# Local attention of layer B: second scores in full PSUM banks, and P times V on 64-key row halves into two banks

## The chip, the cores and the metric

One core of one Trainium2 chip runs the whole program in one launch. The metric is device time in microseconds (us); the median of three runs is given, and one further execution was profiled.

## The reference

Two independent attention layers, each with S = 2048 positions, D = 1024, 32 heads of 32 columns, fp32. Layer A attends to 8 positions at a distance of 2. Layer B is a sliding block:

```
q, k, v = split(x @ wqkv)                        # 32 heads of 32
scores = einsum("bhqd,bhkd->bhqk", q, k) * 32 ** -0.5
mask = (q_idx - k_idx >= 0) & (q_idx - k_idx < 256)
p = softmax(where(mask, scores, -1e9))
o = einsum("bhqk,bhkd->bhqd", p, v)
return o @ wo
```

Both results are concatenated. A query of layer B sees itself and the 255 keys before it.

## The kernel before

The work is cut into eight units of 512 positions: units 0 to 3 are layer B ("dense" in the code), units 4 to 7 layer A. All units but the first of layer B have a halo: the last 256 keys of the unit before. A unit has eight head groups of four heads. Projections (queries and keys L576, values L641, output L702) are accumulations of 24 matmuls in the split of fp32 into a high and a low fp32r part (three products for each of 8 slices); their PSUM banks come from the ring `g`.

For a head group of layer B the scores are computed twice. The first scores (L923, queries on the PSUM partitions) give the maximum and the sum of each row: VectorE masks and takes the maximum (L928), ScalarE exponentiates and sums (L933). Maximum and logarithm of the sum go as an additional row into the stacked queries (L962, L968), so that the second scores (`second`, L1005, keys on the PSUM partitions) come out of exp as finished probabilities. A key block `kb` of 128 keys (-2 to 3, where -2 and -1 are the halo) meets 128, 256 or 384 queries. One bank holds one head's 384 columns, or two heads' 256 or 128; exp (`expo`, L1012) takes a bank to `pbuf` in SBUF, and `keep` zeroes the parts outside the window, on GpSimd (L991) or VectorE (L994), whichever the plan finds earlier. The six key blocks are dealt in two lots, because `pbuf` holds one lot.

P times V (`values`, L1052) follows each lot: plain fp32 matmuls with 128 keys as rows and 32 columns of V, four heads side by side on four column tiles of 32 columns, all accumulating in one bank `o`. After the second lot `finish` splits `o` into a high part (ScalarE, L888) and a low part (VectorE, L892) in the tile `ot`, which the output projection reads one unit later. Layer A's scores and P times V (L772, L838) are computed in a similar way on small tiles.

PSUM has eight banks: `g` 3, scores `s` 4 (`NS`), `o` 1.

The order on every engine is written by a planner inside the kernel. `Clock` keeps the planned end of each engine; four sequences (`gemm`, `ones` for first scores, `twos` for second scores and P times V, `aux`) wait side by side, and the main loop always emits the item whose planned readiness is earliest. Tables steer it: `PACE` (one row for each unit: delays and biases), `V_AT` and `O_AT` (at which head group value parts and output projections of the unit before are placed), `EDGE_AT` with `EDGES_V` (where weights and inputs of the next unit are split at a unit's edge). Weights stream through `raw` buffers by transfers that GpSimd issues (L166), and ScalarE and VectorE split them (L216, L219, L222).

Of the kernel before, what the change touches and what calls it, by code (L numbers as in the profile page):

```python
# [31 lines left out]
PACE = ((0.1, 1.2, 0.1, 0.0, 0.0, -99, 2), (0.2, 1.2, 0.0, 0.0, 0.2, -99, 1), (0.2, 1.2, 0.0, 0.0, 0.0, -99, 2), (0.2, 0.6, 0.0, 0.0, 0.2, -99, 2), (4.0, 7.0, 0.5, 0.0, 1, 2), (4.0, 7.0, 1.5, 0.5, 1, 1), (4.0, 7.0, 0.5, 0.2, 1, 3), (4.0, 7.0, 0.5, 0.0, 1, 2))  # L32
V_AT = ({1: 0, 3: 1, 7: 2}, {0: 0, 5: 1, 7: 2}, {0: 0, 5: 1, 7: 2}, {0: 0, 5: 1, 7: 2}, {0: 0, 5: 1, 7: 2}, {0: 0, 6: 1, 7: 2}, {0: 0, 5: 1, 7: 2}, {0: 0, 5: 1, 7: 2})
O_AT = ({2: (0, 1), 3: (2, 3), 4: (4, 5), 5: (6, 7)}, {2: (0, 1), 3: (2, 3), 4: (4, 5), 5: (6, 7)}, {2: (0, 1), 3: (2, 3), 4: (4, 5), 5: (6, 7)}, {2: (0, 1), 3: (2, 3), 4: (4, 5), 5: (6, 7)}, {2: (0, 1), 3: (2, 3), 4: (4, 5), 5: (6, 7)}, {2: (0, 1), 3: (2, 3), 4: (4, 5), 5: (6, 7)}, {1: (0, 1), 2: (2, 3), 3: (4, 5), 4: (6, 7)}, {2: (0, 1), 3: (2, 3), 4: (4, 5), 6: (6, 7)})
EDGE_AT = (0, 3, 0, 1, 0, 0, 2, 0)
EDGES_V = (
# [207 lines left out]
def kernel(ctx, tc, xs, wqk, wv, wo, outs, units):  # L244
# [175 lines left out]
    class Ring:  # L420
        def __init__(self, pool, n, tag):
            self.pool, self.n, self.tag = pool, n, tag
            self.free = [0.0] * n
            self.i = 0

        def when(self, late=0.0):
            t = self.free[self.i % self.n]
            return t and t + late

        def take(self):  # L430
            i = self.i % self.n
            self.i += 1
            self.free[i] = None
            return self.pool.tile([P, 512], F32, tag=self.tag, name=self.tag), i
# [4 lines left out]
        def empty(self):  # L439
            return None if None in self.free else max(self.free)  # L440

    rg, rs, ro = Ring(psg, 7 - NS, "g"), Ring(pss, NS, "s"), Ring(pso, 1, "o")
# [159 lines left out]
    def v_items(u, part):  # L602
# [64 lines left out]

        for r in range(len(rounds)):
            for n in range(len(rounds[r])):
                for k in range(kw):  # L670
                    for b in range(2):
                        at = (r, n, k, b)
                        out.append((lambda at=at: ready(*at), lambda at=at: run(*at), 3 * (CG if wide else CV),
                                    lambda at=at: after(*at)))
# [223 lines left out]


    def attention(u, s):  # L900
# [80 lines left out]
        kbs = [(-2, 0, 128, 2), (-1, 0, 256, 2)] if has_halo else []  # L981
        kbs += [(0, 0, 384, 1), (1, 128, 384, 1), (2, 256, 256, 2), (3, 384, 128, 2)]
        nk = len(kbs)
        lots = [(0, 1, 2), (3, 4, 5)] if has_halo else [(0, 1), (2, 3)]
        lot = {k: i for i, ks in enumerate(lots) for k in ks}
        at = {k: sum(kbs[i][2] for i in ks if i < k) for ks in lots for k in ks}
# [10 lines left out]
        def second(ki, hp):  # L997
            kb, q0, n, pack = kbs[ki]
            heads = list(range(hp * pack, hp * pack + pack))
            pr = heads[0] // 2  # L1000
            if heads[0] % 2 == 0:
                h["left", ki, pr] = 2 // pack
            ps, bank = rs.take()
            for i, j in enumerate(heads):
                nc.tensor.matmul(ps[:, i * n:(i + 1) * n], kk[:, j, 256 + kb * P:256 + (kb + 1) * P],  # L1005
                                 q[:, j, q0:q0 + n], start=True, stop=True)
            w = pbuf[:, heads[0]:heads[0] + pack, at[ki]:at[ki] + n]
            if ki == nk - 1 and hp == 4 // pack - 1:
                free_keys(hg)

            def expo():
                nc.scalar.activation(w, ps[:, :pack * n].rearrange("p (j n) -> p j n", j=pack),  # L1012
                                     AF.Exp)
                e = ck.use("act", pack * n / 1200 + 0.055, ck.now, pfree[0])
                rs.give(bank, e)

                def masks():
                    r = e
                    if kb >= 0:
                        r = max(r, keep(w[:, :, 0:P], cst["keep_d"], P, pack, 1, 0, -1, e))  # L1020
                    if kb < 2:
                        r = max(r, keep(w[:, :, n - P:n], cst["keep_f"], P, pack, -1, -1, 1, e))
                    h["left", ki, pr] -= 1
# [186 lines left out]
```

## Time and profile before

| | us |
|---|---|
| median of three runs | 1806.58 (1804.88 to 1807.36) |
| span of the profiled execution | 1803.3 |
| TensorE busy in it | 1788.7 |
| VectorE, ScalarE, GpSimd busy | 1229.5, 1036.7, 386.9 |

No separate time of the profiled execution is listed beside its span; the median lies 3.3 us above the span. The profile has rows by source line, engine and operation with their count, busy time and the mean of one; "PE" is TensorE's matmul, "PEld" its weight loads, DVE VectorE, ACT ScalarE, POOL GpSimd. A timeline merges neighbours of one line: start, length, count. An answer by windows counts the instructions that touch a stretch of time.

### The profile page before, as it was taken

To read this page: it belongs to the slowest core of one execution; us is meant where nothing else is said; L and a number is where in the kernel's file an instruction comes from. 1 tells how busy PE (TensorE), PEld (TensorE's weight loads), DVE (VectorE), ACT (ScalarE), POOL (GpSimd) and SP (SyncE) were. 2 spreads that over 40 slices of the span, in tenths; PEclk is the share of its full clock that TensorE was granted. 3 is DMA by queue.
4 is the path that set the end of the run, shared out by engine and by line. 5 is a ranking of instruction groups with operands and counts; after the bars stand their busy time and mean duration, and the time that the engine had idled before them with its cause. 6 is when DMAs were issued, how large, how long until landed. Compare 5 with 4: busy or idle time off the path is not lost.

```text
span 1803.3 us, 34584 instructions
## 1 busy us (share of the span) xinstructions
PE 1788.7 (99%) x12778; PEld 1462.7 (81%) x12778; DVE 1229.5 (68%) x2631; ACT 1036.7 (57%) x2643; POOL 386.9 (21%) x905
## 2 busy tenths in 40 slices
PE   8999999999999999999999999999999999999999
PEld 6787877888787788787888788878888888888887
DVE  6677875657766668666676486686677566866673
ACT  5667667665766665766677364453445344634452
POOL 3222223232232223323233300110001100100000
PEclk9999999999999999999999999999999999999999
DMA  8355665545546455554544433433334443533332
GB/s 243 115 151 136 184 167 148 170 130 172 160 135 177 139 152 176 139 155 134 153 137 138 128 125 125 140 126 135 128 112 151 142 135 113 159 129 135 126 105 82
DMA packets 109129, 257.20 MB, mean 143 GB/s; under 512 B 14496, under 2 KB 29856, under 8 KB 108960
## 3 DMA queue, kind: packets, MB, share of 16 engines
q0 software_dynamic: 41760, 152.06, 26.6%
q1 hardware_dynamic: 56832, 83.00, 17.3%
q10 hardware_dynamic: 10368, 19.93, 3.0%
q8 instruction: 101, 1.65, 0.4%
q14 instruction: 68, 0.56, 0.1%
HBM read 164.63 MB, written 23.07 MB: 104 GB/s over the span
## 4 chain that ended last, share of the span: by engine, by line
PE 94%; DMA 2%; ACT 2%; DVE 2%; issue 0%; POOL 0%; ACTq 0%; SPq 0%; DVEq 0%
PE g L576 38%; PE g L702 19%; PE g L641 18%; PE s L1005 6%; PE s L923 5%; PE o L1052 5%; PE o L838 2%; PE s L772 1%; DMA kst<-nat 1%; DMA halo<-nat 1%; ACT qst L968 1%; DVE s L928 0%; DVE w L222 0%; DMA raw<-xs 0%; ACT kst L391 0%; DMA qst<-nat 0%
## 5 line engine op out<-in xcount | busy, mean ns | idle before, releaser
L576 PE MATMUL g<-x,w 128*128 128x512 f32 x3072 | 763.7, 393 | 2.4 <-ACT x L216 1.3
L576 PEld LDWEIGHTS g<-x,w 128*128 128x128 f32 x3072 | 567.1, 188 | 111.5 <-issue 3.2
L641 PE MATMUL g<-w,x 128*128 128x256 f32 (+1 forms) x2304 | 390.0, 320 | 1.3 <-DVE w L222 1.2
L928 DVE CUSTOM_DVE_ANT_0 s<-s,mask_d 128x384 f32<-128x384 f32 (+2 forms) x512 | 263.2, 553 | 153.5 <-PE s L923 152.3
L222 DVE TENSOR_TENSOR w<-raw,w 128x512 fp32r<-128x512 f32 x516 | 336.6, 694 | 41.1 <-ACT w L216 34.6
L641 PEld LDWEIGHTS g<-w,x 128*128 128x128 f32 x2304 | 333.0, 190 | 30.6 <-DVE w L222 3.2
L702 PE MATMUL g<-ot,w 128*128 128x512 f32 x1416 | 344.0, 393 | 0.9 <-ACT ot L888 0.7
L933 ACT ACTIVATE s<-s,nm 128x384 f32<-128x384 f32 (+2 forms) x512 | 273.5, 535 | 75.0 <-DVE nm L928 72.7
L702 PEld LDWEIGHTS g<-ot,w 128*128 128x128 f32 x1416 | 261.8, 188 | 56.1 <-issue 1.8
L991 POOL TENSOR_SCALAR_AFFINE_SELECT pbuf<-pbuf 128x128 f32<-128x128 f32 (+1 forms) x574 | 205.9, 386 | 267.7 <-ACT pbuf L1012 263.7
L1012 ACT ACTIVATE pbuf<-s 128x384 f32<-128x384 f32 (+2 forms) x480 | 199.5, 506 | 54.7 <-PE s L1005 51.7
L219 DVE CAST w<-raw 128x1024 fp32r<-128x1024 f32 x189 | 130.8, 692 | 76.7 <-PE g L576 44.4
L166 POOL DMA_DIRECT2D raw<-wqk x126 | 68.7, 545 | 458.9 <-DVE w L222 315.8
L923 PE MATMUL s<-kst,qst 96*128 96x384 f32 (+2 forms) x512 | 144.5, 342 | 2.2 <-DMA kst<-nat 1.8
L1005 PEld LDWEIGHTS s<-qst,kst 128*128 128x128 f32 x704 | 108.9, 189 | 36.0 <-ACT s L933 13.2
L1005 PE MATMUL s<-qst,kst 128*128 128x256 f32 (+2 forms) x704 | 132.1, 303 | 1.4 <-ACT qst L968 1.0
L820 ACT COPY wide<-wide 32x256 f32<-32x256 f32 x256 | 103.4, 404 | 38.3 <-DVE wide L811 34.9
L923 PEld LDWEIGHTS s<-kst,qst 96*128 96x128 f32 x512 | 92.4, 188 | 27.2 <-issue 8.1
L166 POOL DMA_DIRECT2D raw<-wv x72 | 46.4, 644 | 279.7 <-DVE w L222 167.9
L933 ACT ACTIVATION_READ_ACCUMULATOR s<-s,nm 128x1 f32 x512 | 104.7, 205 | 0.2
L166 POOL DMA_DIRECT2D raw<-wo x64 | 36.1, 564 | 295.2 <-DVE w L222 158.2
L594 ACT COPY ost<-g 128x512 f32<-128x512 f32 x44 | 25.8, 586 | 120.2 <-PE g L702 120.2
(79 smaller groups left out, 1399.4 us busy)
## 6 DMA issues: line engine op xcount, KB each, us to landing
raw<-wqk POOLq DMA_DIRECT2D x126, 512.0 KB, 3.7
raw<-wv POOLq DMA_DIRECT2D x72, 512.0 KB, 4.2
raw<-wo POOLq DMA_DIRECT2D x64, 512.0 KB, 3.9
qst<-nat SPq DMA_DIRECT2D x96, 256.0 KB, 3.8
kst<-nat SPq DMA_DIRECT2D x96, 256.0 KB, 4.0
raw<-xs POOLq DMA_DIRECT2D x28, 512.0 KB, 4.5
outs<-ost ACTq DMA_DIRECT2D x56, 256.0 KB, 2.2
kst<-halo SPq DMA_DIRECT2D x72, 128.0 KB, 2.7
```

The costliest lines, as they stand in the source:

```text
L166: (self.nc.scalar if early else self.nc.gpsimd).dma_start(raw if len(ap.shape) == 2 else raw.rearrange("p (a b) -> p a b", a=2), ap)
L219: nc.vector.tensor_copy(t[:, 0, :], raw)
L222: nc.vector.tensor_tensor(t[:, 1, c:c + 512], raw[:, c:c + 512], t[:, 0, c:c + 512].bitcast(F32), op=ALU.subtract)
L576: nc.tensor.matmul(h["ps"], h["w"][:, a, k * P:(k + 1) * P], xt[u][k][:, b, :], start=(k == 0 and i == 0), stop=(k == NK - 1 and i == 2))
L641: nc.tensor.matmul(ps, xt[u][kw * g + k][:, a, p0:p0 + P], h["w"][g][:, c, k], start=(first and t == 0 and half == 0), stop=(last and t == 2),
L702: nc.tensor.matmul(h["ps"], w[:, a, c:c + P], ot[u, k][:, b, :], start=(k == 0 and i == 0), stop=(k == NK - 1 and i == 2))
L923: nc.tensor.matmul(ps[:, :n], q[0:96, j, b * P:(b + 1) * P], kk[0:96, j, c0:c1], start=True, stop=True)
L928: nc.vector.tensor_tensor_reduce(ps[:, :n], ps[:, :n], mask[:, cut:full], scale=-1.0, scalar=BIG, op0=ALU.add, op1=ALU.min, accum_out=nm)
L933: nc.scalar.activation(ps[:, :n], ps[:, :n], AF.Exp, bias=nm, scale=-1.0, accum_out=sm)
L991: nc.gpsimd.affine_select(w, w, pattern=[[0, m], [step, n]], compare_op=ALU.is_ge, fill=0.0, base=base, channel_multiplier=chan)
L1005: nc.tensor.matmul(ps[:, i * n:(i + 1) * n], kk[:, j, 256 + kb * P:256 + (kb + 1) * P], q[:, j, q0:q0 + n], start=True, stop=True)
L1012: nc.scalar.activation(w, ps[:, :pack * n].rearrange("p (j n) -> p j n", j=pack), AF.Exp)
```

## The change

`second` now fills whole banks: for a head, the 128 or 384 columns of two key blocks stand next to each other in one bank of 512 (blocks -2 and 0 in the first lot, 3 and 1 in the second), and the 256 columns of two heads share a bank (block 2 in the first lot, block -1 in the second). One exp covers a bank. Where two masked squares of 128 columns of one kind lie in the bank, one mask instruction covers both by a strided view. The number of matmuls and their columns stay.

`values` works on 64 keys at a time: the row half r (keys 0 to 63 or 64 to 127 of a block) uses rows 64r to 64r+63 of the array, covers only the 320 query columns that its keys can see (fewer at the edges), and accumulates in a bank of its own (`o` for r = 0, `x` for r = 1). A list alternates the halves so that both get the same number of columns; heads 0 and 1 go through the whole list first, then heads 2 and 3. `join` replaces `finish` in layer B: ScalarE copies `x` into `pbuf` (the columns of head 3), VectorE adds `o`, then ScalarE and VectorE split the sum as before. The last exp of the next group's first lot, which is head 3's, is planned behind that.

The ring `g` has two banks while layer B runs; at its end the bank of `x` joins it. The value projection lets its second bank lag by two steps in layer B (`SKEW`), so that the two banks finish at different times. The planner's cost of P times V follows the new columns. The tables have new entries: `PACE` in units 1 to 5 and 7, `V_AT` in unit 4, `O_AT` in units 4 and 6, `EDGE_AT` in units 1 to 4, two rows of `EDGES_V`; `LAG7` is used by no unit.

```diff
-LAG7, LAG0 = 1, 3
+LAG7, LAG0 = 0, 3
+SKEW = 2
...
-EDGE_AT = (0, 3, 0, 1, 0, 0, 2, 0)
+EDGE_AT = (0, 1, 2, 0, 1, 0, 2, 0)
...
-    psg = ctx.enter_context(tc.tile_pool(name="psg", bufs=7 - NS, space=PSUM))
+    psg = ctx.enter_context(tc.tile_pool(name="psg", bufs=2, space=PSUM))
+    psx = ctx.enter_context(tc.tile_pool(name="psx", bufs=1, space=PSUM))
...
+        skew = SKEW if units[u][2] else 0
         for r in range(len(rounds)):
+            steps = [(n, k) for n in range(len(rounds[r])) for k in range(kw)]
+            for i in range(len(steps) + skew):
+                for b in range(2):
+                    if 0 <= i - skew * b < len(steps):
+                        at = (r,) + steps[i - skew * b] + (b,)
...
+    def join(u, s, h):
...
+        both = pbuf[:, 3, :S]
+        nc.scalar.copy(both, h["o"][1])
...
+            nc.vector.tensor_tensor(both, h["o"][0], both, op=ALU.add)
...
+                nc.scalar.copy(o[:, 0, :], both)
...
+                    nc.vector.tensor_tensor(o[:, 1, :], both, o[:, 0, :].bitcast(F32), op=ALU.subtract)
...
-        lots = [(0, 1, 2), (3, 4, 5)] if has_halo else [(0, 1), (2, 3)]
+        lots = [[((0, 128, 384),), ((2, 512, 256),)], [((3, 0, 128), (1, 128, 384))]]
+        if has_halo:
+            lots = [[((-2, 0, 128), (0, 128, 384)), ((2, 512, 256),)], [((3, 0, 128), (1, 128, 384)), ((-1, 512, 256),)]]
+        lots = [[(segs, (j,)) for j in range(3) for segs in lot[:1]] +
+                [(segs, (j, j + 1)) for j in (0, 2) for segs in lot[1:]] +
+                [(segs, (3,)) for segs in lot[:1]] for lot in lots]
...
             for i, j in enumerate(heads):
+                for kb, c, w in segs:
+                    q0 = max(0, kb * P)
+                    x = i * n + c - c0
+                    nc.tensor.matmul(ps[:, x:x + w], kk[:, j, 256 + kb * P:256 + (kb + 1) * P], q[:, j, q0:q0 + w],
+                                     start=True, stop=True)
...
+                for r in range(2):
+                    a, b = max(0, kb * P + 64 * r if has_halo or kb else 0), min(S, kb * P + 64 * r + 320)
+                    p.append((b - a, r, kb, a, c + a - q0))
+            rows_of = [sorted(x for x in p if x[1] == r) for r in range(2)]
+            out, t = [], [0, 0]
+            while rows_of[0] or rows_of[1]:
+                r = 0 if rows_of[0] and (not rows_of[1] or t[0] <= t[1]) else 1
+                out.append(rows_of[r].pop())
+                t[r] += out[-1][0]
...
-                for j in range(4):
-                    nc.tensor.matmul(h["o"][32 * j:32 * j + 32, q0:q0 + n],
-                                     v[:, slot, vc + 32 * j:vc + 32 * j + 32], pbuf[:, j, at[ki]:at[ki] + n],
-                                     start=(ki == 0), stop=(ki == nk - 1), skip_group_check=True)
+            for j0 in (0, 2):
+                for n, r, kb, q0, c in pieces[li][0]:
+                    slot = (4 * u + kb) % 6
+                    part = slice(64 * r, 64 * r + 64)
+                    for j in (j0, j0 + 1):
+                        nc.tensor.matmul(h["o"][r][32 * j:32 * j + 32, q0:q0 + n],
+                                         v[part, slot, vc + 32 * j:vc + 32 * j + 32], pbuf[part, j, c:c + n],
+                                         start=(j, r) not in h["begun"], stop=True, skip_group_check=True)
```

More of the change, by code (lines that the diff above doesn't have):

```diff
@@ L995, in keep, with second @@
             return ck.use("dve", dur_d, r, port=True)
[L997 to L1002, printed above, removed]
+        def second(li, ci):
+            segs, heads = lots[li][ci]
+            m = len(heads)
+            c0, n = segs[0][1], sum(x[2] for x in segs)
             ps, bank = rs.take()
             for i, j in enumerate(heads):
[L1005 to L1008, printed above, removed]
+                for kb, c, w in segs:
[3 more added lines that the diff above has]
+                                     start=True, stop=True)
+            w = pbuf[:, heads[0]:heads[0] + m, c0:c0 + n]
+            if li == 1 and ci == len(lots[1]) - 1:
@@ new lines, in attention @@
+        for lot in lots:
+            p = []
+            for kb, c, w in [x for segs, heads in lot for x in segs if heads[0] == 0]:
+                q0 = max(0, kb * P)
+                for r in range(2):
[7 more added lines that the diff above has]
+                t[r] += out[-1][0]
+            pieces.append((out, max(t)))
```

127 lines of the change are left out of this document (70 added, 57 removed), and 4 rows, old and new, of the table EDGES_V.

## The prediction

> **What bounds the kernel now.** I read the page's busy times first, then busy time by stage, then the chain of waits.
>
> ```profile
> span 1803.3 us, 34584 instructions
> PE 1788.7 (99%) x12778; PEld 1462.7 (81%) x12778; DVE 1229.5 (68%) x2631; ACT 1036.7 (57%) x2643; POOL 386.9 (21%) x905
> PE 94%; DMA 2%; ACT 2%; DVE 2%; issue 0%; POOL 0%; ACTq 0%; SPq 0%; DVEq 0%
> ```
> ```profile
> core 0: us, PE busy (x), PEclk, DMA share, GB/s
> 0.00:45.00 45.00, 39.63 (x163) 1.00 0.81 242
> 45.00:1030.00 985.00, 980.09 (x6005) 1.00 0.52 149
> 1030.00:1803.00 773.00, 769.01 (x6613) 1.00 0.39 128
> ```
>
> TensorE is busy 99% of the span at the full granted clock (1.00), and 94% of the chain is its own work. Layer B ends about 1030 us. Between 45 and 1030 us TensorE idles 985.0 - 980.1 = 4.9 us, in layer A 4.0 us. No other engine is a bound on average. So the change must be costed as TensorE time that goes or comes, plus a few microseconds of waits. The span is 1803.3 us; the median of the runs is 1806.58, 3.3 us above it, and I add that 3.3 to every sum.
>
> **Part 1, P times V.** This is the only part that changes TensorE's work: the first scores, the second scores (same 704 matmuls, same columns), and the projections keep their matmuls.
>
> ```profile
> 63.66 1.50 PE L1052 MATMUL o<-pbuf,vbuf 128*32 128x384 f32 x16
> 70.40 0.86 PE L1052 MATMUL o<-pbuf,vbuf 128*32 128x256 f32 x16
> 406.32 1.50 PE L1052 MATMUL o<-pbuf,vbuf 128*32 128x384 f32 x24
> ```
>
> Each source matmul is two MATMULs (704 in the loop, 1408 in the trace), and four heads run side by side on four column tiles. In the first unit the burst at 63.66 us has 384+384 = 768 columns for each head, the one at 70.40 has 256+128 = 384. The slope is (1.50 - 0.86)/384 = 1.67 ns per column for four heads together. Each of the 48 lots in units with a halo (24 head groups, two lots) has 768 columns, as the third row; the 8 groups of the first unit have 768+384 = 1152.
>
> After the change a piece covers 64 keys and only the 320 columns that those keys can see. By the greedy list, each row half gets 640 columns a lot with a halo, and 576+448 = 1024 for a group without. If both row halves and all four heads run at once, a lot with a halo falls from 768 to 640 columns, 128 x 1.67 = 0.21 us, times 48 is 10.2 us; the first unit gains 128 x 1.67 x 8 = 1.7 us. That is the good end: -11.9 us.
>
> But the loop does heads 0 and 1 through the whole list before heads 2 and 3. If only the four tiles of one pair ran at a time, a lot would take 2 x 640 columns: +512 x 1.67 = 0.85 us, times 48 is 41.0, and the first unit (2048 - 1152) x 1.67 x 8 = 11.9: +52.9 us, the bad end. What decides is how far the array looks past matmuls that wait for their own tile. The nearest rows are those of the scores of layer A, 32 source matmuls on eight tiles (32 rows by 64 columns), in one burst, counted from its start:
>
> ```profile
> 1080.03:1080.13 0.10, 0.10 (x8) 0.10 (x11) 1.00 0.96 266
> 1080.03:1080.23 0.20, 0.20 (x18) 0.20 (x26) 1.00 1.15 297
> 1080.03:1080.33 0.30, 0.30 (x27) 0.30 (x33) 1.00 0.97 280
> 1080.03:1080.39 0.36, 0.36 (x33) 0.36 (x34) 1.00 1.00 302
> 1080.03:1080.48 0.45, 0.45 (x38) 0.45 (x41) 1.00 0.97 305
> 1080.03:1080.63 0.60, 0.60 (x52) 0.60 (x58) 1.00 0.91 304
> 1080.03:1080.98 0.95, 0.95 (x64) 0.80 (x64) 1.00 0.84 295
> ```
> ```profile
> L772 PE MATMUL s<-pbuf x2048: 221/221/272, 1034.4 to 1750.8; 32*64 32x72 f32 x187
> ```
>
> The first column in brackets is MATMULs begun, the second weight loads. Eight begin within 0.10 us, one on each tile: eight tiles in four row groups and two column groups do run together. 33 loads have begun by 0.30 us, and then only one more by 0.36: after 16 source matmuls (32 loads, 32 MATMULs) the stock in front of the array is used up and the rest is fed as earlier ones finish. Eight rounds of 72 columns need 8 x 72 x 0.83 = 0.48 us (0.83 is half the slope, for one of the two MATMULs); the burst took 0.95, and 0.73 without the last MATMUL's own 0.22. So what lies beyond the first 16 cost 0.25 us here.
>
> In a lot with a halo of the changed kernel, heads 0 and 1 make 12 source matmuls and heads 2 and 3 the next 12. The stock of 16 reaches the first four of the second pair, so all eight tiles start, but the list outruns it. I charge the same 0.25 us to each of the 48 lots: -0.21 + 0.25 = +0.04, +1.9 us in all. The first unit's lots have 16 source matmuls and are not charged: -1.7 us. Sum: **+0.2 us**, with -11.9 and +52.9 as ends. Entering and leaving the small tiles happens twice a group as before. The sum trusts that the 0.25 comes from the queue and not from the tile size.
>
> *A rule that speaks against the change.* Twice as many MATMULs must be fed. From 0.36 to 0.60 us the rows count 52 - 33 = 19 MATMULs, 12.6 ns each; 96 of them are 1.2 us, less than the 1.32 us of a lot in my sum, so by the rows feeding adds nothing. The Trainium skill, TensorE: Matmul & The Clock Gate, section Back-to-back issue gap, gives a floor of about 25 ns for each MATMUL however small; by it a lot of 96 would take 2.4 us and the kernel would end some 64 us later (an estimate from that page). This trace disagrees with the floor for tiles that run together.
>
> **Part 2, exp, masks and the join.**
>
> ```profile
> L1012 ACT ACTIVATE pbuf<-s 128x384 f32<-128x384 f32 x256 | 108.1, 508 | 33.5 <-PE s L1005 33.0
> L1012 ACT ACTIVATE pbuf<-s 128x512 f32<-128x512 f32 x112 | 63.2, 610 | 12.6 <-PE s L1005 10.6 <-POOL pbuf L991 1.3
> L1012 ACT ACTIVATE pbuf<-s 128x256 f32<-128x256 f32 x112 | 39.1, 396 | 8.6 <-PE s L1005 8.1 <-POOL pbuf L991 0.5
> L991 POOL TENSOR_SCALAR_AFFINE_SELECT pbuf<-pbuf 128x128 f32<-128x128 f32 x397 | 129.2, 354 | 125.0 <-ACT pbuf L1012 122.9 <-PE s L1005 0.8
> L991 POOL TENSOR_SCALAR_AFFINE_SELECT pbuf<-pbuf 128x256 f32<-128x256 f32 x177 | 77.8, 456 | 142.7 <-ACT pbuf L1012 140.8
> L888 ACT CAST ot<-o 128x512 fp32r<-128x512 f32 x64 | 37.5, 587 | 98.2 <-PE o L1052 56.1 <-PE o L838 41.6
> L892 DVE TENSOR_TENSOR ot<-o,ot 128x512 fp32r<-128x512 f32 x64 | 43.9, 686 | 69.2 <-ACT ot L888 69.1
> ```
>
> Exp goes from 16 to 12 instructions in a group with a halo, from 12 to 10 in one without: 480 to 368, of which 336 have 512 columns and 32 have 384. By the means 256 x 0.508 + 112 x 0.610 + 112 x 0.396 = 242.7 us becomes 336 x 0.610 + 32 x 0.508 = 221.2: -21.5 on ScalarE. The join adds one copy of 0.587 in each of 32 groups, +18.8, and one VectorE add, priced like the subtraction, 32 x 0.686 = +22.0. Masks fall from 24 to 20 in a group with a halo and from 20 to 18 in the first unit: 512 narrow and 224 wide become 288 and 336, at GpSimd's means 283 to 255 us, -28 over GpSimd and VectorE. ScalarE gains 2.7, VectorE and GpSimd together 6: nothing for an engine at 57% or 68%.
>
> The join's chain is four steps (0.587 + 0.686 + 0.587 + 0.686 = 2.5 us) instead of two. Nobody near waits for `ot`: the output projection of a unit runs in the unit behind. Head 3's exp of the next group's first lot now waits for the join, since the join borrows its columns; it stands last in the lot, behind five other banks of exp (five of 0.61 = 3.1 us), which cover the 2.5. Without that cover TensorE would turn to projections, and the loss is at most 2.5 us in each of 31 groups, 78 us, if it found none.
>
> ```profile
> PEld s L1005 <- ACT s L933: 13.2, 24, 0.6
> ```
>
> The second scores' weight loads waited 13.2 us in total, 24 times, for a score bank in which the exp of the first scores still ran. In a group with a halo the four score banks now turn 29 times (16 first, 12 second, 1 for the row sums) instead of 33. Such waits come only where the ring is tight, so the gain lies between an eighth of the row, 1.6, and more than all of it is worth, the 8.9 us that TensorE idles behind 45 us. I take a third of the row: **-4.4 us**. On the other side a bank is held for 0.610 instead of 0.508 us; if all 336 wide exps were waited for, 336 x 0.10 = +34, but 24 waits among 480 exps say few are, and 24 x 0.10 = 2.4 is the loss I keep.
>
> **Part 3, two banks for the projections, and the tables.**
>
> ```profile
> L513 ACT ACTIVATE nat<-g 128x512 fp32r<-128x512 f32 x64 | 38.3, 598 | 71.0 <-PE g L576 69.0 <-DMA qst<-nat 1.4
> L517 DVE SCALAR_TENSOR_TENSOR nat<-g,nat 128x512 fp32r<-128x512 f32 x64 | 44.0, 688 | 52.1 <-ACT nat L513 52.0
> L594 ACT COPY vbuf<-g 128x512 f32<-128x512 f32 x44 | 25.6, 586 | 48.9 <-PE g L641 47.1
> 1302.52 22.00 PE g L576 x96
> ```
>
> In layer B the ring `g` has two banks instead of three. A query or key accumulation is 24 matmuls of 22.00/96 = 0.229 us, 5.5 us, and its bank must be empty one accumulation later; the copy out is 0.598 + 0.688 = 1.3 us. Covered. The value rounds fill two banks at once; the skew of two steps lets the first bank finish 2 x 3 x 0.229 = 1.4 us ahead of the second, against a copy of 0.586. Covered unless something stands ahead on ScalarE or VectorE. The tables move the places of weight splits, value parts and edge loads in most units; number and size of the transfers stay, GpSimd issues them with the masks as now. I price the tables at nothing: TensorE idles so little that a new fit has at most the 8.9 us above to win.
>
> **Sum of the likeliest case:** 1803.3 + 3.3 + 0.2 - 4.4 = 1802.4 us. Its own range is 1797 to 1808.
>
> **Rivals.** (1) *All eight tiles stay filled.* The stock is renewed in time and the 0.25 us falls away: -11.9, with none or all of the 4.4: 1790 to 1795. For it: pieces of 64 to 384 columns take longer than those of 72, so feeding is less pressed. Against: the stock renews as matmuls finish, and these finish later too.
>
> (2) *Value rounds wait for their bank.* There are 16 rounds in layer B (32 of the 64 copies). From the point where two other instructions (0.6 us each) stand ahead of the copy, it ends 0.586 + 1.2 + about 0.2 for the hand-off = 2.0 us after the last matmul, 0.6 later than the skew covers: 16 x 0.6 = 10 us, with no gain elsewhere 1806.6 + 10 = 1817; at half that 1811. For it: a third bank held this today. Against: ScalarE and VectorE are 57% and 68% busy, so two ahead is not the rule.
>
> (3) *One pair of heads at a time.* 1806.6 + 52.9 = 1859 us. Against it are the counts above, where eight begin before any of them can have finished. The same page of the Trainium skill, section The mechanism, says that MATMULs start and end strictly in program order; by that rule heads 2 and 3 could not start before heads 0 and 1 are through, which is this rival. The bursts above disagree with it: four heads' MATMULs of 384 columns, each head's two next to each other in the program, share the 1.50 us.
>
> (4) *Nothing moves*: gain and loss cancel, 1805 to 1808.
>
> (5) *Feeding bounds a lot.* If a MATMUL took twice the 12.6 ns, a lot of 96 would take 2.4 us against 1.28, and 48 x 1.1 = 54 us would come on top, 1860 us. Against it is the same count of 19.
>
> **Chances.** Forecast 0.52, (1) 0.18, (2) 0.21, (3) 0.05, (4) 0.03, (5) 0.01. About 0.2% (3.6 us) is what a measurement of this kernel can tell from no change: faster is below 1803.0, slower above 1810.2. The forecast's range lies 0.27 on the faster side, 0.23 within, 0.02 beyond (waits of the third part). Faster: 0.27 + 0.18 = 0.45; same: 0.23 + 0.03 = 0.26; slower: 0.02 + 0.21 + 0.05 + 0.01 = 0.29. The range runs from the full overlap to the value rounds' wait, 1790 to 1817; it leaves out (3), (5) and the tails of the others.
>
> **What would show it.** The P times V bursts of 96 MATMULs: 1.45 to 1.6 us confirms the forecast, 1.25 to 1.35 rival (1), above 2.2 rival (3) or (5). Loads of the second scores waiting for ScalarE: below 13.2 us, or the second term is wrong. TensorE idle ahead of the value matmuls in layer B, 0.6 us at a time, would be rival (2). A change of more than 4 us in layer A, where only tables move, would make the third part wrong.

## The result, and the profile after

| | before | changed |
|---|---|---|
| median (us) | 1806.97 (1804.88 to 1810.01, 4 runs) | 1832.34 (1830.10 to 1834.56, 4 runs) |
| span of the profiled execution | 1803.3 | 1831.4 |
| P times V in it | 88.2 | 106.0 |

The changed kernel is slower by 1.43%: ratio 1.0143, 95% interval 1.0128 to 1.0157. The forecast was 1802.4, range 1790 to 1817. From the page of the changed kernel:

```profile
span 1831.4 us, 37311 instructions
PE 1809.4 (99%) x14186; PEld 1504.5 (82%) x14186; DVE 1245.9 (68%) x2632; ACT 1034.4 (56%) x2552; POOL 370.2 (20%) x835
PE 87%; DMA 4%; DVE 3%; issue 3%; ACT 2%; SPq 0%; POOL 0%; ACTq 0%; POOLq 0%; DVEq 0%
```

TensorE is as full as before (99%), so it received more work or its work became longer; the chain lost 7 points of TensorE (94% to 87%), so waits came too. Both show by stage. The last P times V matmul begins at 1046.4 us after the first matmul, against 1021.7 (+24.7); what follows, layer A, grew by 3.4. The same stretch of layer B by windows, first before, then changed:

```profile
45.00:1020.00 975.00, 971.00 (x5954) 788.13 (x5953) 658.14 (x1788) 649.32 (x1780) 292.18 (x718) 1.00 0.52 149
```
```profile
45.00:1020.00 975.00, 964.22 (x7131) 805.33 (x7131) 657.59 (x1762) 637.33 (x1673) 263.30 (x625) 1.00 0.52 147
```

The columns after the length are busy time of PE, PEld, DVE, ACT, POOL. TensorE idles 10.8 us here instead of 4.0. To split the rest I charged every MATMUL of the trace with the time until the next one starts (so with the wait behind it too), and summed by kind. The spans of the two profiled executions differ by 28.1 us. Of these, P times V **+17.8** us, value projections +5.3, second scores +2.8, layer A's scores +1.5, first scores +0.8, output projections +0.8, queries and keys 0.0. Nearly two thirds of the loss are in P times V.

One lot with a halo of the changed kernel, counted from its first MATMUL by windows of L1109 alone (PE busy with MATMULs begun, then weight loads):

```profile
275.71:275.76 0.05, 0.05 (x4) 0.05 (x8) 1.00 0.97 369
275.71:275.99 0.28, 0.28 (x4) 0.15 (x8) 1.00 0.73 271
275.71:276.10 0.39, 0.39 (x8) 0.25 (x12) 1.00 0.55 205
275.71:276.27 0.56, 0.56 (x8) 0.28 (x12) 1.00 0.39 143
275.71:276.30 0.59, 0.59 (x12) 0.30 (x16) 1.00 0.37 135
275.71:276.37 0.66, 0.66 (x16) 0.37 (x24) 1.00 0.33 121
275.71:277.53 1.82, 1.82 (x48) 1.31 (x48) 1.00 0.12 44
```

Four MATMULs begin at once (heads 0 and 1, both row halves) and then nothing new for 0.28 us: four of the eight tiles stand empty. Between 0.28 and 0.39 the second pass of the same four starts, between 0.56 and 0.59 the second piece of heads 0 and 1, and heads 2 and 3 begin only behind that, at 0.59 to 0.60 us in all 48 lots. "99% busy" hides this: a TensorE with half its tiles at work counts as busy. The lot takes 1.82 us; counted to the start of what follows, all 48 take 1.804 to 1.818, against 1.433 (median) before.

The waits on the scores and the stacked keys, after:

```profile
PEld s L1043 <- ACT s L969: 2.4, 8, 0.3
PEld s L959 <- ACT s L969: 4.4, 13, 0.7
PE s L959 <- DMA kst<-nat: 6.4, 4, 3.1
```

The loads of the second scores wait 2.4 us for ScalarE instead of 13.2, as forecast. But the first scores (L959) now wait 6.4 us for their stacked keys, where the kernel before waited 1.8.

### The profile page after: what moved, and what is told of

Read it like the earlier page. It is cut to its first block, busy times and chain, and to the rows that moved or that the text cites. A ratio compares the mean times of both kernels' runs of the same rounds, so it can differ in the third digit from the quotient of the medians.

```text
span 1831.4 us, 37311 instructions
## 1 busy us (share of the span) xinstructions
PE 1809.4 (99%) x14186; PEld 1504.5 (82%) x14186; DVE 1245.9 (68%) x2632; ACT 1034.4 (56%) x2552; POOL 370.2 (20%) x835
## 4 chain that ended last, share of the span: by engine, by line
PE 87%; DMA 4%; DVE 3%; issue 3%; ACT 2%; SPq 0%; POOL 0%; ACTq 0%; POOLq 0%; DVEq 0%
PE g L579 29%; PE g L707 15%; PE g L644 13%; PE x L579 6%; PE s L1043 6%; PE s L959 5%; PE o L1109 4%; PE x L707 3%; PE x L644 3%; PE o L843 2%; PE x L1109 1%; PE s L777 1%; DMA kst<-nat 1%; DMA raw<-wqk 1%; DVE w L219 1%
## 5 line engine op out<-in xcount | busy, mean ns | idle before, releaser
L579 PE MATMUL g<-x,w 128*128 128x512 f32 x2544 | 632.0, 393 | 1.8 <-ACT x L213 1.3
L579 PEld LDWEIGHTS g<-x,w 128*128 128x128 f32 x2544 | 473.0, 189 | 93.3 <-ACT x L213 1.8
L644 PEld LDWEIGHTS g<-w,x 128*128 128x128 f32 x1920 | 283.9, 190 | 25.7 <-DVE w L219 2.4
L1028 POOL TENSOR_SCALAR_AFFINE_SELECT pbuf<-pbuf 128x256 f32<-128x256 f32 (+1 forms) x504 | 189.3, 405 | 255.5 <-ACT pbuf L1050 237.2
L1050 ACT ACTIVATE pbuf<-s 128x512 f32<-128x512 f32 (+1 forms) x368 | 188.4, 601 | 82.0 <-PE s L1043 81.8
L959 PE MATMUL s<-kst,qst 96*128 96x384 f32 (+2 forms) x512 | 143.2, 340 | 9.4 <-DMA kst<-nat 6.4
L579 PE MATMUL x<-x,w 128*128 128x512 f32 x528 | 127.2, 393 | 0.0
L1043 PE MATMUL s<-qst,kst 128*128 128x128 f32 (+2 forms) x704 | 125.1, 307 | 1.6 <-ACT qst L1004 1.2
L959 PEld LDWEIGHTS s<-kst,qst 96*128 96x128 f32 x512 | 92.3, 189 | 32.5 <-issue 6.0
L579 PEld LDWEIGHTS x<-x,w 128*128 128x128 f32 x528 | 97.9, 188 | 21.8 <-issue 1.2
L1109 PE MATMUL o<-pbuf,vbuf 64*32 64x320 f32 (+4 forms) x1408 | 109.7, 351 | 0.0
L1109 PE MATMUL x<-pbuf,vbuf 64*32 64x320 f32 (+5 forms) x1408 | 109.0, 349 | 0.0
```

The lines of the kernel that those rows point to most:

```text
L579: nc.tensor.matmul(h["ps"], h["w"][:, a, k * P:(k + 1) * P], xt[u][k][:, b, :], start=(k == 0 and i == 0), stop=(k == NK - 1 and i == 2))
L644: nc.tensor.matmul(ps, xt[u][kw * g + k][:, a, p0:p0 + P], h["w"][g][:, c, k], start=(first and t == 0 and half == 0), stop=(last and t == 2),
L959: nc.tensor.matmul(ps[:, :n], q[0:96, j, b * P:(b + 1) * P], kk[0:96, j, c0:c1], start=True, stop=True)
L1028: nc.gpsimd.affine_select(w, w, pattern=[[0, m], [step, n]], compare_op=ALU.is_ge, fill=0.0, base=base, channel_multiplier=chan)
L1043: nc.tensor.matmul(ps[:, x:x + w], kk[:, j, 256 + kb * P:256 + (kb + 1) * P], q[:, j, q0:q0 + w], start=True, stop=True)
L1050: nc.scalar.activation(w, ps[:, :m * n].rearrange("p (j n) -> p j n", j=m), AF.Exp)
```

## The experiments

The theory after this result: (T) a tile takes in two source matmuls, and a third one for the same tile stops everything behind it; so the order "heads 0 and 1 through the whole list" keeps half of the array empty. Its rivals were (R1) that 64-row tiles are slow in any order, and (R2) that the loss is outside P times V: one projection bank less, the new tables, or the full banks. All runs in one table; "layer B" is the move of the last P times V start, "P×V" the sum of start to start, both of the one profiled execution of each kernel and against that of the kernel before.

| run | median us | ratio (95%) | layer B | P×V |
|---|---|---|---|---|
| all4 | 1810.67 | 1.0030 (1.0017 to 1.0043) | +5.4 | -10.6 |
| cut4 (one time) | 1820.09 | | +11.9 | +1.6 |
| cut5 (one time) | 1835.23 | | +26.9 | +17.2 |
| pv128 | 1828.98 | 1.0127 (1.0107 to 1.0148) | +16.4 | -0.6 |
| pv128b3 | 1830.24 | 1.0128 (1.0112 to 1.0143) | +17.6 | -1.4 |
| oldtables | 1857.55 | 1.0289 (1.0272 to 1.0306) | +33.8 | +19.5 |
| newtables | 1808.52 | 1.0010 (1.0001 to 1.0020) | +3.4 | 0.0 |
| second | 1816.40 | 1.0058 (1.0043 to 1.0073) | +0.6 | +0.4 |
| banks | 1835.06 | 1.0158 (1.0141 to 1.0175) | +29.3 | +0.6 |
| banks0 | 1823.55 | 1.0100 (1.0085 to 1.0115) | +14.4 | 0.0 |
| skewonly | 1827.91 | 1.0124 (1.0109 to 1.0139) | +22.2 | +0.6 |
| pvonly | 1834.56 | 1.0150 (1.0135 to 1.0165) | +22.5 | -2.0 |
| all4ns3 | 1879.50 | 1.0402 (1.0385 to 1.0420) | +62.7 | +0.2 |
| all4s0 | 1833.47 | 1.0150 (1.0133 to 1.0166) | +27.8 | -6.7 |
| all4ahead | 1842.75 | 1.0200 (1.0185 to 1.0216) | +33.4 | -9.1 |
| replan | 1807.51 | 1.0004 (0.9995 to 1.0013) | +1.8 | 0.0 |
| all4e0 | 1810.69 | 1.0022 (1.0010 to 1.0034) | -0.3 | -10.6 |
| all4e02 | 1814.99 | 1.0050 (1.0031 to 1.0068) | +9.3 | -10.5 |

### The order of the heads in P times V

**all4**: all four heads on each piece.

```diff
-            for j0 in (0, 2):
+            for js in ((0, 1, 2, 3),):
...
-                    for j in (j0, j0 + 1):
+                    for j in js:
```

> The changed kernel, with the P times V loop taking all four heads for each 64-key piece before the next piece, instead of heads 0 and 1 through the whole list and then heads 2 and 3. Same matmuls, same columns. Theory 1 (the array looks past waiting matmuls only a short way, so heads 2 and 3 start late in lots of 24 source matmuls): a lot with a halo falls from 1.81 us to about 1.3 us, all eight tiles begin within 0.1 us, and the kernel ends near 1832 - 48 x 0.5 = 1808 us. Theory 2 (64-row tiles, or two row halves at once, are slow by themselves): the lots stay near 1.8 us and the kernel near 1832 us.

1810.67 us: some 21 us of the loss are gone by an exchange of loops, though P times V fell by 28.4 (+17.8 to -10.6). A lot by the same kind of windows:

```profile
280.46:280.51 0.05, 0.05 (x8) 0.05 (x13) 1.00 0.65 246
280.46:281.05 0.59, 0.59 (x21) 0.36 (x29) 1.00 0.30 108
280.46:281.70 1.24, 1.24 (x48) 0.85 (x48) 1.00 0.15 55
```

All eight tiles begin within 0.05 us; 21 MATMULs have begun at 0.59, where the changed kernel had 12. All 48 lots take 1.241 to 1.244 us. The 1.811 of the changed kernel is this 1.242 plus the 0.57 us by which heads 2 and 3 begin late (0.59 to 0.60 instead of 0.01 to 0.03). R1 falls. R2 does not fall with it: outside P times V layer B stands 16.0 us above before (5.4 + 10.6), where the changed kernel had 6.9 (24.7 - 17.8). The value projections' sum rose to +9.9, and the waits for stacked keys from 6.4 to 7.9 us. A likely reason, which no run isolates, is that the time in which half of the array stood empty was also time for ScalarE, VectorE and the transfers, so that some of their work is late when it goes. The 16.0 belongs to one execution, 3.2 us above the median of its kernel; all4e0 below, with the same median, has 10.3 in one that lies 3.7 us under it.

Part of it is the clock. In this execution of all4 four waits of TensorE, of 1.3 to 3.0 us, are each followed within 2 us by 3.4 us at a granted clock of 0.50. The wait for the stacked keys at the end of unit 0, and what follows it, by windows (PE busy with MATMULs, then the clock):

```profile
186.74:189.77 3.03, 0.07 (x1) 1.00 1.07 326
189.77:193.18 3.41, 3.41 (x16) 0.50 0.79 273
```

Half the clock for 3.41 us is 1.7 us of work. By this estimate, in which nothing but TensorE's work sets the time of such a stretch, all4 lost 6.8 us in four such stretches, the changed kernel 1.7 in one (near 11 us), and the profiled execution of the kernel before, at 1.00 throughout, nothing. By it, some 5 of the 9 us between 16.0 and 6.9 are the clock behind waits, and not the waits themselves.

**cut4** and **cut5**: heads 0 and 1 do the first four (five) pieces, then heads 2 and 3 the same, then both pairs the rest. Thus heads 2 and 3 begin as the 9th (11th) source matmul instead of the 13th.

```diff
-            for j0 in (0, 2):
-                for n, r, kb, q0, c in pieces[li][0]:
+            cut = 4
+            runs = [(j0, g) for g in (pieces[li][0][:cut], pieces[li][0][cut:]) for j0 in (0, 2)]
+            for j0, g in runs:
+                for n, r, kb, q0, c in g:
```

> The changed kernel, with the list of pieces of a lot cut after 4 of its 6 pieces: heads 0 and 1 through the first 4, heads 2 and 3 through the first 4, then the same for the last 2. Heads 2 and 3 so begin at the 9th source matmul instead of the 13th. Theory 1a (what stops the array is a third piece of the same tile waiting ahead; the first unit's lots, where heads 2 and 3 also begin at the 9th and start 0.05 us in, show it): eight tiles within 0.1 us and lots of about 1.25 to 1.35 us, as with all four heads for each piece. Theory 1b (the order by pairs costs as such, by sharing something between the pair's halves): lots stay above 1.6 us.

> As before but cut after 5 of 6 pieces: heads 2 and 3 begin at the 11th source matmul, one row half has its third piece ahead of them. Theory 1a: a late start again, after the second pieces have begun (near 0.3 to 0.6 us), lots between 1.35 and 1.8 us. A theory that counts instructions of any tile up to 64 (16 source matmuls) expects a start within 0.1 us and 1.25 to 1.35 us.

With four pieces ahead, two on each tile of heads 0 and 1, heads 2 and 3 begin after 0.053 us in all 48 lots. The rows of cut4: 7 and 8 MATMULs stand where the changed kernel had 4.

```profile
277.48:277.55 0.07, 0.07 (x7) 0.07 (x11) 1.00 0.93 351
277.48:277.76 0.28, 0.28 (x8) 0.21 (x16) 1.00 0.71 264
277.48:279.00 1.52, 1.52 (x48) 1.10 (x48) 1.00 0.14 51
```

With five pieces, the fifth being the third of its tiles, they begin at 0.575 to 0.588 us and a lot takes 1.79 to 1.805. Two source matmuls more ahead cost 0.53 us of start. A limit on how many MATMULs may wait does not explain it: in cut4 12 of them wait ahead of heads 2 and 3, which begin all the same, and in cut5 too no more than 12 wait from 0.32 us on, yet they do not begin. The third one on a tile explains it: it enters when the first is through, at 0.56 us. So the starts confirm T. The lengths do not follow from it alone: a lot of cut4 takes 1.43 to 1.52 us, neither the 1.25 to 1.35 expected nor the 1.24 of all4. Its last MATMUL begins at 1.28 to 1.32 us, where all4's begins at 1.07 to 1.10; what holds back the end of these lots stays open.

### The other parts, one at a time

**pv128**: the changed kernel with P times V on 128 keys in one bank and `finish` instead of the join (its `x` bank idle in layer B). **pv128b3**: that bank given back to `g`.

```diff
-            for j0 in (0, 2):
-                for n, r, kb, q0, c in pieces[li][0]:
+            for kb, c, w in [x for segs, heads in lots[li] for x in segs if heads[0] == 0]:
...
-                    join(u, s, h)
+                    finish(u, s, h)
```
```diff
-    psg = ctx.enter_context(tc.tile_pool(name="psg", bufs=2, space=PSUM))
+    psg = ctx.enter_context(tc.tile_pool(name="psg", bufs=3, space=PSUM))
```

> The changed kernel with P times V taken back to 128 keys in one bank and the old finish (no join), everything else of the change kept: second scores in full banks, two projection banks in layer B, the skew, the new tables. Theory 1 (P times V costs 18 of the 25 us): lots at 1.43 us again and the kernel near 1832 - 18 = 1814 us, the remaining 7 us being second scores, tables and banks. Theory 3 (the two projection banks, the tables or the join cost the time, and the P times V bursts only show it): near 1830 us without the join's share.

> The changed kernel with its full-bank second scores and its tables, but P times V on 128 keys in one bank as before, and the bank so left over given to the projections (three banks g in layer B). The same with two banks and the eighth one idle ran 1828.98. If the missing third projection bank is the cost there, most of the 22 us above the kernel before go: 1806 to 1813, with value and first-score time back by 9 and 6 us. If the tables are the cost, whatever the banks, it stays at 1820 to 1830.

The lots are back at 1.43 us, but the kernel gains only 3.4: 16.4 us remain in layer B, 17.0 of them outside P times V. So the +17.8 is time inside the lots, and how much of it the kernel gets back depends on what takes its place: 28.4 us less in P times V brought some 21 in all4, 18.4 less bring 3.4 here. The third bank changes nothing (1830.24 against 1828.98), so the reading that the missing bank is the cost here, put down before pv128b3, fell. But pv128b3 keeps the skew, which costs 22.4 us with three banks by itself (skewonly below), so this pair does not tell bank from skew.

**oldtables**: the changed kernel with all tables of before. **newtables**: the kernel before with all tables of the changed one.

```diff
-EDGE_AT = (0, 1, 2, 0, 1, 0, 2, 0)
+EDGE_AT = (0, 3, 0, 1, 0, 0, 2, 0)
... and PACE, V_AT, O_AT, EDGES_V, LAG7
```

> The changed kernel with all load tables as they were before the change. Theory 1: P times V bursts stay at 1.81 us, the total within some 6 us of the changed kernel's 1832, either way, as the tables decide only some waits. Theory 4 (the new tables are what costs): near 1812 us or below.

> The kernel before with nothing but the tables of the changed kernel. If the tables only fit two banks g better than the old ones do, they bring nothing here: 1805 to 1815. If they are a better plan in themselves (they are worth 25 us in the changed kernel), the time falls to 1785 to 1795. The prediction priced them at nothing, within 8.9 us: 1798 to 1815.

The new tables are worth 25.2 us in the changed kernel (1857.55 against 1832.34) and cost 1.6 in the kernel before. They are no better plan in themselves; they repair what the other edits do.

**second**: the kernel before with full-bank second scores alone. **banks**: the kernel before with two banks `g` in layer B and the skew; **banks0**: the two banks without the skew; **skewonly**: the skew with three banks. **pvonly**: the kernel before with P times V on row halves in the order of all4, the join, two banks and the skew. All five with the old tables. All but skewonly also hold a small edit of the planner, which the changed kernel does not have and no run has alone: a stacking job may not pass an older one that waits (`hg - 2 not in waiting`).

```diff
# banks, banks0
-    psg = ctx.enter_context(tc.tile_pool(name="psg", bufs=7 - NS, space=PSUM))
+    psg = ctx.enter_context(tc.tile_pool(name="psg", bufs=2, space=PSUM))
+    psx = ctx.enter_context(tc.tile_pool(name="psx", bufs=1, space=PSUM))
# skewonly (banks the same, with SKEW = 2 as a constant)
+        skew = 2 if units[u][2] else 0
+            for i in range(len(steps) + skew):
```

> The kernel before with the second scores in full banks as the only change of work: P times V with 128 keys, the old finish, three projection banks, no skew, the tables from before. In the planner a late job now waits behind one that stands before it. Theory 1: matmuls unchanged, the second scores take at most 3 us more or less, 1803 to 1812 us. Theory 5 (wider exps make the score banks late): above 1815 us, with weight loads of the second scores waiting for ScalarE.

> The kernel before with two projection banks instead of three in layer B and the skew of the value rounds, nothing else (the eighth bank is unused in layer B). It prices what the second bank for P times V takes away. Theory 6 (two banks cost waits): 1812 us or more, with TensorE waiting ahead of value matmuls or query and key accumulations. Theory 1 with banks free of cost: 1804 to 1810 us. Tables that were fitted to three banks may add a few us in either.

> The kernel before with only P times V changed: 64-key halves in two banks with all four heads for each piece, the join, two projection banks, the skew; second scores in the old banks (head 3's in the first lot last), tables from before. If the P times V gain carries over, 10 us less in its bursts; if banks, join and unfitted tables cost as much as they did around the first such order (15 us), 1806 to 1815 us.

> The kernel before with two banks g in layer B and without the skew (with the skew 1835.06). If the skew was most of that cost, 1810 to 1820. If the missing bank is the cost, 1830 to 1845.

> The kernel before with nothing but the skew of two steps in the value rounds of layer B (three banks g, old tables). If the skew by itself makes weight splits late: 1812 to 1818, with the value matmuls 6 to 10 us longer. If it only costs together with two banks: 1804 to 1810.

Several of the ranges set beforehand failed: oldtables, pvonly and skewonly lie above both of theirs, banks0 between its two, and `second` has the time of its theory 5 without the waits that this named (its second scores wait 7.8 us for ScalarE, less than before).

Full banks bring nothing: layer B +0.6; most of what is lost lies in layer A (+8.3 of 9.0 us in the span), which this edit does not touch except through the plan. Against the runs of the kernel before beside them (1805.49 and 1806.77), the bank alone costs 18.1 us, the skew alone 22.4, both 28.3: they do not add up. What they share stands in the waits of the two kinds of scores for a score bank, skewonly first, then banks0:

```profile
PEld s L1007 <- ACT s L935: 15.5, 31, 0.8
PEld s L925 <- ACT s L935: 14.4, 30, 1.7
PE s L925 <- ACT s L935: 5.7, 8, 1.4
PE g L641 <- DVE w L222: 2.6, 5, 0.8
```
```profile
PEld s L1016 <- ACT s L944: 13.4, 27, 0.8
PEld s L934 <- ACT s L944: 6.6, 16, 0.9
PE g L648 <- DVE nat L524: 2.0, 4, 0.7
```

Before, the loads of the second scores waited 13.2 us for ScalarE, and the first scores 1.5 by their loads. With the skew the first scores (L925) wait 14.4 us by their loads and 5.7 us by their matmuls, for the exp of the first scores ahead. The value projections themselves wait for little: 2.6 us for weight splits with the skew, 2.0 us for a copy of `nat` with two banks. So a change in the projections shows as waits of the scores; that this is so because both share ScalarE and VectorE is a reading, and no run parts it from the order of the plan. In time the losses of skewonly come in steps: the same first-score matmul begins 12.3 us later than before all the way from 296 to 380 us, 17.5 from 585 to 602 and 23.1 from 861 to 893 (from the start of the span). Within a unit the offset often stands still; it moves most around the edges of units, where value rounds, splits of the next unit and its first scores meet.

pvonly has the order of all4, and yet P times V gains 2.0 us and not 10.6. Its lots take 1.32 to 1.35 us. In the old lots the blocks -2, -1 and 0 give one row half 704 columns and the other 576, where the lots of the changed kernel give 640 to each; 64 columns more at 1.67 ns are 0.11 us. So the pairing of blocks that came with the full banks also serves P times V, and the two parts of the change cannot be priced apart.

**replan**: the kernel before with one planned cost changed, so that only the order shifts.

```diff
-C1, C3, CG, CV = 0.108, 0.2, 0.231, 0.242
+C1, C3, CG, CV = 0.108, 0.25, 0.231, 0.242
```

> The kernel before with one planned cost changed: C3, the planner's allowance for each lot of P times V, 0.25 instead of 0.2. Every instruction, bank and table stays; only the order between the sequences shifts. If the tables fit one plan only, and that is what the missing bank, the skew and the full banks each lost by (10 to 22 us), the time rises by 5 to 20 us: 1811 to 1826. If those edits cost what they cost by themselves, it stays within 3 us: 1804 to 1809.

1807.51: no change. So my suspicion that any order the tables were not fitted to costs 5 to 20 us does not hold for this shift. It is a weak test: by the traces, TensorE's order differs from the kernel before at 97 of 12778 MATMULs here and at 2542 in skewonly. Whether the bank and the skew have prices of their own, or cost what a larger shift of the plan costs, is not shown.

### Trying for a version that beats both

**all4ns3**: all4 with three banks `s` and three banks `g` in layer B. **all4s0**: all4 with SKEW = 0. **all4ahead**: all4 with the next weight's split planned as soon as the first bank has begun a block. **all4e0**, **all4e02**: all4 with the edge row of before for unit 0, and for units 0 and 2.

```diff
# all4ns3
-NRAW, NP, NS = 3, 768, 4
+NRAW, NP, NS = 3, 768, 3
-    psg = ctx.enter_context(tc.tile_pool(name="psg", bufs=2, space=PSUM))
+    psg = ctx.enter_context(tc.tile_pool(name="psg", bufs=3, space=PSUM))
# all4s0
-SKEW = 2
+SKEW = 0
# all4ahead
-                if k == 0 and b == 1 and n < 3:
+                if k == 0 and b == early and n < 3:
# all4e0 / all4e02: rows 4 and 5 are the rows 0 and 2 of before
-EDGE_AT = (0, 1, 2, 0, 1, 0, 2, 0)
+EDGE_AT = (4, 1, 2, 0, 1, 0, 2, 0)
+EDGE_AT = (4, 1, 5, 0, 1, 0, 2, 0)
```

> The changed kernel with all four heads on each piece (that alone ran 1810.67), and the eighth bank taken from the scores instead of from the projections: three banks s and three banks g in layer B; the bank x joins the scores for layer A. If the lost projection bank is what eats the 10.6 us that P times V gains, and the scores can spare one bank, 1796 to 1803. If the scores need their four banks, TensorE waits for exp in many head groups: 1815 to 1850.

> The changed kernel with all four heads on each piece (1810.67 with the skew) and with SKEW = 0, so the value rounds fill their two banks in step as before. The skew lets the first bank ask for the next weight two steps before the second bank issues the split of that weight: the look-ahead over the splits is gone. If that is what makes the value projections 9 us longer, the time falls to 1798 to 1804, below the kernel before. If two banks without the skew wait for their copies, as rival (2) of the prediction had it, 1815 to 1825.

> As all4 with the skew kept, but the split of the next weight is planned when the first bank, not the second, has begun the block: the look-ahead is back and the copies stay apart. If the late splits are the cost, 1799 to 1806. If the splits were never late, 1808 to 1814 as with all4.

> The changed kernel with all four heads on each piece (1810.67), and unit 0 with the edge row of before (value part and x at places 10 and 17 instead of 7 and 14). If the early value part is what makes the stacked keys late at the end of unit 0 (3.1 us), 1806 to 1810. If the plan behind it shifts as in the other unfitted runs, 1815 to 1830.

> As all4e0, and unit 2 with its edge row of before too (last x part at 28 instead of 31), where all4 loses 2.7 us at the start of unit 3. If both stalls go, 1802 to 1808. If the plan shifts, 1815 to 1835.

all4ns3, all4s0 and all4ahead lie above every range set for them. The scores need their four banks: with three, TensorE's first scores alone wait 11.5 us for exp, and 73 us are lost against the kernel before. Taking the skew away costs 22.8 us with the two banks and the new tables, so it is not a mistake there. Earlier splits cost 32 us against all4, though TensorE's waits for weight splits fell from 2.4 to 0.4 us:

```profile
PE s L959 <- DMA kst<-nat: 11.7, 5, 5.0
PE s L959 <- ACT s L969: 7.9, 6, 4.3
PE s L959 <- issue: 4.6, 4, 1.8
```

The waits moved to the stacked keys and the score banks, and the clock went with them: by the estimate above, stretches at 0.50 cost all4ahead 17 us and all4ns3 26. all4e0 equals all4, and all4e02 at 1814.99 is slower than it; the wait for stacked keys at the end of unit 0 stayed (4.9 us in the profiled execution, 3.0 in that of all4), so the early value part is not its cause. What makes these keys late was not settled: in all4 the last of the six stacking transfers there is issued at 183.1 us, and the keys' three take 6.3 us (median) to land, against 5.2 in the kernel before. No version with P times V on row halves beat the kernel before; all4 and all4e0, at 1.0030 and 1.0022, come nearest.

## Why the prediction was wrong

**Part 1, the look-ahead (the step that failed).** It read the burst of layer A's scores as "a stock of 16 source matmuls", whatever their tile, and concluded that all eight tiles start. But that burst had eight tiles in turn, so 16 source matmuls are two on each tile, and the 17th is the first third one on a tile. The rows could not tell the two readings apart; I should have kept both, with 12 source matmuls on four tiles ahead of heads 2 and 3 as the case that parts them. By the right reading the price could have been worked out from rows: heads 2 and 3 wait for two passes of 320 columns, 2 x 320 x 0.83 = 0.53 us. Measured, the step's +0.04 us for a lot is +0.38 (1.811 against 1.433), times 48 = 18.1; the first unit's 16 lots, where heads 2 and 3 stand 9th in the program, give about -0.3 together instead of -1.7 (without the few lots, before and after, that hold a wait); sum +17.8 where the text had +0.2. The ends held: all4's -10.6 is near the good end -11.9, and +17.8 is a third of the way to +52.9. The true case lay between the forecast and rival (3): the pairs overlap after 0.60 us, and the range left that out.

**The count of MATMULs.** The text gave a lot 96 MATMULs. 24 source matmuls are 48, as the rows above show. So its check on feeding was twice too strict: 48 at 12.6 ns are 0.6 us, and even at the 25 ns of the rule that it weighed they are 1.2 us, under the 1.32 of its sum, so that neither the 64 us nor rival (5) had a ground. The conclusion, that feeding does not bound a lot, stands: eight begin in 0.05 us in all4. The bursts' length was to decide: 1.45 to 1.6 us forecast, 1.25 to 1.35 rival (1), above 2.2 rivals (3) and (5). 1.81 lies in none of them.

**Strict program order.** The prediction set a rule of the Trainium skill (TensorE: Matmul & The Clock Gate, section The mechanism: MATMULs start and end in program order) against this trace and let the trace decide. The runs do not bear the rule out: starts are not in program order, since in the changed kernel heads 2 and 3 begin at 0.59 to 0.60 us and the third pieces of heads 0 and 1, which stand ahead of them, only from 0.89 on. But a tile's third source matmul does hold back what follows, so the rule's warning, which the prediction set aside, had a real case behind it.

**Part 2.** The wait of 13.2 us fell to 2.4, as said, but not a third of it was gained: the second scores take 2.8 us more, and `second` alone leaves layer B at +0.6. The row was a wait of weight loads, behind which TensorE was mostly still busy with the matmul ahead; TensorE idled only 4.0 us from 45 to 1020 us (975.00 less 971.00). By these runs the term is not below 0, where the text had -4.4. The exp count and price came as worked out:

```profile
L1050 ACT ACTIVATE pbuf<-s 128x512 f32<-128x512 f32 x336 | 175.0, 610 | 81.3 <-PE s L1043 81.2
L910 ACT COPY pbuf<-x 128x512 f32<-128x512 f32 x32 | 18.8, 587 | 60.6 <-PE x L1109 60.6
L915 DVE TENSOR_TENSOR pbuf<-o,pbuf 128x512 f32<-128x512 f32 x32 | 22.0, 687 | 11.2 <-ACT pbuf L910 11.2
```

336 at 0.610 us, a copy at 0.587 and an add at 0.687 are the prices in the text, and the join hides as it said: no wait of TensorE in the changed kernel names it.

**Part 3.** "Covered" and "at most 8.9 us" were wrong. The cover was computed for each accumulation by itself, as was rival (2)'s wait of the value rounds; the cost came at another place, in first scores waiting for exp (skewonly) and in stalls around unit edges: 18.1 us for the bank and 22.4 for the skew with the old tables, each with the shift of the plan that it brings. The tables win 25.2 back, far over the bound I drew from the idle time of the kernel before. That bound holds for a plan that fits (newtables: +1.6); it says nothing on what tables save once an edit has spoiled the fit. Layer A moved by 3.4, inside the 4 us of the text, and so did not show the fault. In the changed kernel this part and the second cost 6.9 us of layer B, and 10 to 17 in the profiled executions of all4e0, all4 and pv128, which have the same banks, skew and full banks: by the medians they eat the whole 10.6 us that a good order of P times V gains, and that is why rival (1), right on the lots in all4 (1.24 us), would not have had its 1790 to 1795. How these 10 to 17 us divide among bank, skew, full banks and the clock behind the waits stays open, since the single edits do not add up; the waits and the clock shown are as far as the runs lead.

## What to carry to other kernels

When small tiles run side by side on the array, write the loop over tiles innermost: never put three matmuls for one tile ahead of the first for another (seen here with plain fp32 on tiles of 64 rows by 32 columns). A busy share of 99% does not show empty tiles; count how many MATMULs begin in the first 0.1 us of a burst. And a bound such as "the idle time is 8.9 us, so a new order wins at most that" is valid only for the program it was read from: price a lost bank or a shifted accumulation at the place where its neighbours on the shared engines wait, not by its own cover. Look at the granted clock behind each wait too: in all4 a wait of 3.0 us cost some 1.7 us more.

## What the runs showed of the hardware

A tile of 64 rows by 32 columns takes in two source matmuls ahead (four MATMULs: 704 fp32 source matmuls are 1408 in the trace before); the third blocks the queue for all tiles until the first is through: heads 2 and 3 begin at 0.053 us as 9th source matmul, at 0.575 to 0.588 as 11th and at 0.59 to 0.60 as 13th. Eight such tiles in two row halves run at the same time almost without loss: a lot of 48 MATMULs with 640 columns for each row half takes 1.24 us, against 1.43 for 768 columns on four tiles of 128 rows (128 columns less at 1.67 ns would be 1.22). In all4, waits of TensorE of 1.3 to 3.0 us were followed by 3.4 us at a granted clock of 0.50.
